# Shorter VectorE code, five transfers for the last values and 24 pad matmuls in a DMA-bound decode attention kernel

## The chip, the cores and the metric

The kernel runs on 1 core of one Trainium2 chip. The metric is the device time of one execution in microseconds (us). The kernel before takes 441.15 us (median of 3 runs, 440.98 to 441.19).

Engines: PE does matmuls (PEld is its weight load), DVE is VectorE, ACT is ScalarE, POOL is GpSimd, SP issues most of the transfers.

## The reference

Two attention blocks of a decode step, A and B: 4 sequences, 1 new token, 32 query heads on 8 key/value heads of 128, 8192 cached positions. A attends to all positions, B to the last 2048. The outputs are joined.

```python
q = (x @ wq).reshape(B, Sq, Hq, Dh).transpose(0, 2, 1, 3)      # D = 512, Hq*Dh = 4096
k, v = repeat(k_cache, 4), repeat(v_cache, 4)                   # B: only the last 2048 positions
p = softmax(einsum("bhqd,bhkd->bhqk", q, k) * Dh ** -0.5)
out = einsum("bhqk,bhkd->bhqd", p, v).reshape(B, Sq, Hq * Dh) @ wo
```

Everything is bf16. The caches of A are 2 x 64 MB and the used part of B's is 2 x 16 MB, so some 184 MB have to come in from memory for little arithmetic.

## The kernel before

The work is 20 units: 4 for B, then 16 for A, each with 4 MB of keys and 4 MB of values. PE transposes a unit's keys, computes scores, and runs the PV product of the unit before it. Two units make a turn; PE's code for a turn stands once, in a loop of 10 turns. DVE and ACT have their first three turns unrolled and then a loop. The last unit's PV and the last part of the output projection stand behind the loop (the tail).

At the start DVE sets masks and evacuates the small matmuls that make q:

```python
        def pe_job_xT(P):
            idx = xt_idx[P] = new_job("xT", "dve")
            ...
            def efn(dve):
                return dve.tensor_copy(out=xT[:, P, :, :],
                                       in_=bk[:, 0:DC * 8].rearrange("p (c b) -> p c b", c=DC)[:, :, 0:Bn])
        # pe_job_QP: one copy per job, 8 jobs.  pe_job_perm: four copies per job, 2 jobs.   (cut)

        def dve_setup0(dve):            # 4 memsets of MK; dve_setup1: 4 of MASK[0]; dve_setup2: 4 copies for permE
            mkv = MK[:, :].rearrange("p (g s h) -> p g s h", g=NSEG, s=2)
            dve.memset(mkv[0:64, :, 0, :], 0.0)
            ...
        op("dve", dve_setup0, inc=("mk0",))
```

POOL clears buffers and makes the identity matrices, which release PE's first instruction. Each step of DVE's softmax chain has a semaphore of its own (`max`, `maxc`, `sum`, `rcp`, `os`), on which later DVE steps wait.

The tail; each `c` is 16 matmuls of the last unit L:

```python
        VCH = [4, 2, 1, 1]                                  # V of the last unit in four transfers: 2, 1, 0.5, 0.5 MB
        vch_of = [i for i, n in enumerate(VCH) for _ in range(n)]
        for c in range(NC):                                 # NC = 8
            w = [("VL", vch_of[c])]
            if c == 0:
                w.append(("exp", L, 0))
            if c == 4:
                pe_SM(L)                                    # 16 matmuls for the softmax sums
                op("pe", pe_seed, waits=[("ocp", NTURN - 1)])
            pe_PV(L, c, bank=KTB[0], waits=w)
        add_norm(L, bank=KTB[0])
        # then 16 projection matmuls, two for each of eight 128 KB loads of Wl, which come last in the queue
```

Of the kernel before, what the change touches and what calls it, by code (L numbers as in the profile page):

```python
# [9 lines left out]
ACTF = mybir.ActivationFunctionType  # L10
# [4 lines left out]
def bass_concat_heads__gqa_block_cached__sliding_block_cached__decode_kernel(  # L15
# [15 lines left out]
    Bn, _, D = A_x.shape  # L31
    _, HKV, SK, DH = A_k_cache.shape
# [6 lines left out]
    NSEG = 4  # L39
# [31 lines left out]
    with ExitStack() as es:  # L71
# [8 lines left out]
        def sm(name):  # L80
# [39 lines left out]
        KTB = [ps("KT%d" % i, 512) for i in range(NBK)]  # L120
        OTB = ps("OT", 512)

        names = ["k0", "k1", "kh", "v0", "v1", "vl0", "vl1", "vl2", "vl3", "wl0", "wl1", "wl2", "wl3", "wl4", "wl5", "wl6", "wl7", "x0", "x1", "w0", "w1", "wo",
                 "out0", "out1", "out2", "Tq", "Td", "Ta", "S", "PV", "Ed", "Ea", "Eq", "max", "sub", "sum", "rcp", "exp", "otr", "os", "otp",
                 "ocp", "Ef", "fin0", "fin1", "ar1", "SM", "maxc", "pset", "setup", "pm0", "pm1", "oc", "ocB", "mk0", "mk", "mka", "perm", "rq"]
        sems = {n: sm("s_" + n) for n in names}

        K_sbf = K_sb.bitcast(F32)
# [6 lines left out]
        def sem_of(key):  # L135
            t = key[0]
            if t in ("K", "Kh"):
                return sems["k%d" % (key[1] % 2)]
            if t in ("V", "Vh"):
                return sems["v%d" % (key[1] % 2)]  # L140
            if t == "T":
                j = jobs[key[1]]
                return sems["Tq" if j["turn"] is None else "Td" if j["eng"] == "dve" else "Ta"]
            if t == "pm":
                return sems["pm%d" % key[2]]
            if t == "KH":
                return sems["kh"]
            if t in ("VL", "WL", "x", "out", "fin"):
                return sems["%s%d" % (t.lower(), key[1])]
            if t == "WQ":  # L150
                return sems["w%d" % key[1]]
            if t == "E":
                if jobs[key[1]]["turn"] is None:
                    return sems["Eq"]
                return sems["Ed"] if jobs[key[1]]["eng"] == "dve" else sems["Ea"]
            return sems[t]

        DMA_KEYS = ("K", "Kh", "KH", "V", "Vh", "VL", "WL", "x", "out", "WQ", "wo", "mk")

# [10 lines left out]
        def add(d):  # L170
            op(d["eng"], d["fn"], waits=d["waits"], inc=d["inc"])
# [16 lines left out]
            return KTB[jobs[idx]["bank"]]  # L188

        def pe_job_xT(P):  # L190
            idx = xt_idx[P] = new_job("xT", "dve")
            bk = kbank(idx).bitcast(BF16)

            def fn(pe):
                ins = None
                for c in range(DC):
                    ins = pe.transpose(out=bk[:, c * 8:c * 8 + Bn], in_=x_sb[0:Bn, P, :].rearrange("b (p c) -> b c p", c=DC)[:, c, :],  # L197
                                       identity=ident[0:Bn, 0:Bn])
                return ins
            op("pe", fn, waits=[("x", P), ("setup",), bankfree(idx)], inc=("T", idx))  # L200

            def efn(dve):
                return dve.tensor_copy(out=xT[:, P, :, :],
                                       in_=bk[:, 0:DC * 8].rearrange("p (c b) -> p c b", c=DC)[:, :, 0:Bn])
            add(dict(eng="dve", fn=efn, waits=[("T", idx)], inc=("E", idx)))

        def wq_view(P):
            return V_sb[:, 1 - P, :, :].rearrange("p t d -> p (t d)").rearrange("p (c n) -> p c n", c=DC)

        def pe_job_QP(P, i):  # L210
            idx = qp_idx[(P, i)] = new_job("QP", "dve")
            bk = kbank(idx)
            wv = wq_view(P)

            def fn(pe):
                ins = None
                for hl in range(HQJ):
                    hq = i * HQJ + hl
                    for c in range(DC):
                        ins = pe.matmul(out=bk[:, hl * Bn:(hl + 1) * Bn], lhsT=wv[:, c, hq * DH:(hq + 1) * DH],  # L220
                                        rhs=xT[:, P, c, :], start=(c == 0), stop=(c == DC - 1))
                return ins
            op("pe", fn, waits=[("WQ", P), ("E", xt_idx[P]), bankfree(idx)], inc=("T", idx))

            def efn(dve):
                return dve.tensor_copy(out=QT[:, P, :, i * HQJ:(i + 1) * HQJ],
                                       in_=bk[:, 0:HQJ * Bn].rearrange("p (h b) -> p b h", b=Bn))
            add(dict(eng="dve", fn=efn, waits=[("T", idx)], inc=("E", idx)))

        def pe_job_perm(P):  # L230
            idx = perm_idx[P] = new_job("perm", "dve")
            bk = kbank(idx)

            def fn(pe):
                ins = None
                for e in range(2):
                    ins = pe.matmul(out=bk[:, e * Bn * HQ:(e + 1) * Bn * HQ],
                                    lhsT=permE[:, e, :, :].rearrange("p t i -> p (t i)"),
                                    rhs=QT[:, P, :, :].rearrange("p b h -> p (b h)"), start=True, stop=True)
                return ins  # L240
            op("pe", fn, waits=[("E", qp_idx[(P, NQP - 1)]), ("perm",), bankfree(idx)], inc=("T", idx))

            def efn(dve):
                ins = None
                for e in range(2):
                    for tl in range(2):
                        src = bk[64 * tl:64 * tl + 64, e * Bn * HQ:(e + 1) * Bn * HQ]
                        ins = dve.tensor_copy(
                            out=RQ[P][64 * tl:64 * tl + 64, :, :, e, C * tl:C * tl + C],
                            in_=src.rearrange("p (b g c) -> p b g c", b=Bn, g=NSEG))  # L250
                return ins
            add(dict(eng="dve", fn=efn, waits=[("T", idx)], inc=("E", idx)))

        def pe_filler(n):
            bank = (jobs[-1]["bank"] + 1) % NBK
# [103 lines left out]
        def pe_job_OL(tn):  # L359
            idx = ol_idx[tn] = new_job("OL", "dve")  # L360
            bk = kbank(idx)

            def fn(pe):
                ins = None
                for r in range(REP):
                    ins = pe.matmul(out=bk[:, r * NR:(r + 1) * NR], lhsT=ORx[:, r, :, :].rearrange("p h m -> p (h m)"),
                                    rhs=ident[0:NR, 0:NR], start=True, stop=True)
                return ins
            op("pe", fn, waits=[("E", ot_idx[tn]), bankfree(idx)], inc=("T", idx))

            def efn(dve):
                ins = None
                for h in range(REP):
                    ins = dve.tensor_copy(
                        out=OL[32 * h:32 * h + 32, :, :, :],
                        in_=bk[32 * h:32 * h + 32, 0:REP * NR].rearrange("p (r g h b) -> p g h r b", r=REP, g=2, h=REP)[:, :, h, :, :])
                return ins
            return dict(eng="dve", fn=efn, waits=[("T", idx)], inc=("E", idx))
# [125 lines left out]
        def pool_otp(tn):  # L504
# [5 lines left out]
                w.append(("otr", 2 * tn - 2))  # L510
            return dict(eng="pool", fn=lambda pool: pool.tensor_copy(out=OTp[:, :, :], in_=OT_sb[:, P, q, :, :]), waits=w, inc=("otp", tn))

        def pool_setup0(pool):
            pool.memset(dummy[:, :], 0.0)
            pool.memset(onesf[:, :], 1.0)
# [4 lines left out]
            pool.memset(oacc[:, :], 0.0)  # L520
            pool.memset(PT[:, :, :], 0.0)
            return pool.memset(Wo_sb[:, :, :, :], 0.0)
        op("pool", pool_setup0, inc=("pset",))

        def pool_setup1(pool):
            ins = pool.affine_select(out=ident[:, :], in_=onesb[:, :], pattern=[[1, 128]],
# [3 lines left out]
            return ins  # L530
        op("pool", pool_setup1, waits=[("pset",)], inc=("setup",))

        def dve_setup0(dve):
            mkv = MK[:, :].rearrange("p (g s h) -> p g s h", g=NSEG, s=2)
            dve.memset(mkv[0:64, :, 0, :], 0.0)
            dve.memset(mkv[0:64, :, 1, :], -BIG)
            dve.memset(mkv[64:128, :, 0, :], -BIG)
            return dve.memset(mkv[64:128, :, 1, :], 0.0)
        op("dve", dve_setup0, inc=("mk0",))

        def dve_setup1(dve):
            dve.memset(MASK[0][0:64, 0:REP], 0.0)
            dve.memset(MASK[0][0:64, REP:C], -BIG)
            dve.memset(MASK[0][64:128, 0:REP], -BIG)
            return dve.memset(MASK[0][64:128, REP:C], 0.0)
        op("dve", dve_setup1, inc=("mka",))

        def dve_setup2(dve):
            ins = None
            for e in range(2):  # L550
                for tl in range(2):
                    ins = dve.tensor_copy(out=permE[:, e, tl, :], in_=ident[:, :].rearrange("p (i e) -> p e i", e=2)[:, e, :])
            return ins
        op("dve", dve_setup2, waits=[("setup",)], inc=("perm",))
        for sh in range(2):
            m0 = MASK[1][:, :]
            pstm = m0.ap[0][0]
# [13 lines left out]
        def act_warm(act):  # L571
            return act.activation(out=dummy[:, 1:2], in_=dummy[:, 0:1], func=ACTF.Exp)
        op("act", act_warm, waits=[("setup",)])

        for P in (1, 0):
            pe_job_xT(P)
# [102 lines left out]
            return ins  # L679
        add(dve_sum(L))  # L680
        add(dve_rcp(L))
        VCH = [4, 2, 1, 1]
        vch_of = [i for i, n in enumerate(VCH) for _ in range(n)]
        for c in range(NC):
            w = [("VL", vch_of[c])]
# [246 lines left out]
```

## Time and profile before

| | value |
|---|---|
| time, median of 3 | 441.15 us |
| span of the profiled run | 439.6 us |
| bytes, mean rate over the span | 184.76 MB, 420 GB/s |
| DMA rate from 200 to 300 us | 431 GB/s |
| busy share PE, DVE, ACT | 83%, 48%, 43% |
| idle of PE between the loop and the tail | 1.36 us |
| stall of PE among the last projections (start to start, less the usual 0.11 us) | 0.66 us |

Lines of the page of before: busy time by engine (us, share, instructions), the DMA packets, the chain of work that ended last by engine, and two lines of the DMA issues (count, KB each, median us from issue to landing).

```profile
PE 365.9 (83%) x7302; PEld 338.4 (77%) x7312; DVE 210.1 (48%) x462; ACT 189.7 (43%) x203; POOL 27.8 (6%) x84
...
DMA packets 13253, 184.76 MB, mean 420 GB/s; under 512 B 1412, under 2 KB 2488, under 8 KB 4536
...
DMA 46%; PE 45%; PEld 4%; issue 2%; DVE 1%; SPq 1%; PEldq 0%
...
K_sb<-in_A_k_cache_dram SPq DMA_DIRECT2D x15, 4096.0 KB, 22.8
V_sb<-in_A_v_cache_dram SPq DMA_DIRECT2D x15, 4096.0 KB, 30.6
```

PE, DVE and ACT all have idle time. The 4 MB loads land 22.8 and 30.6 us after issue; at 430 GB/s (an estimate from the table below) 4 MB take 9.8 us, so each load waits in a filled queue.

The table of stretches of before: for each stretch its length, busy us and instruction count of PE, PEld, DVE, ACT and POOL, granted PE clock, DMA share, GB/s.

```profile
core 0: us, PE busy (x) PEld busy (x) DVE busy (x) ACT busy (x) POOL busy (x), PEclk, DMA share, GB/s
40.00:100.00 60.00, 57.46 (x1177) 53.89 (x1179) 33.64 (x65) 33.78 (x36) 2.24 (x7) 1.00 1.02 424
...
200.00:300.00 100.00, 84.77 (x1620) 79.30 (x1619) 49.41 (x106) 45.02 (x48) 4.39 (x17) 0.91 1.00 431
...
430.00:440.00 10.00, 6.63 (x141) 4.90 (x137) 1.22 (x4) 0.37 (x1) 0.00 (x0) 1.00 0.49 173
```

The DMA engines run at a share of 1.00 to 1.02 from 40 to 400 us.

The timeline of before at the start (start us, us, engine, line, instruction, and in brackets the idle time before it and what ended that): the issue of the first V loads, and PE's first transpose of keys.

```profile
24.33 4.81 SPq L566 DMA_DIRECT2D V_sb<-in_B_v_cache_dram  x4
...
34.54 3.28 PEld L278 LDWEIGHTS KT<-identf,K_sb 128*128 128x128 f32 x16 [4.01 <-DMA K_sb<-in_B_k_cache_dram]
```

PE waits 4 us for the first keys, so the startup chain has that much to spare.

The timeline of PE in the tail of before: the last unit's PV (x64 are 64 matmuls), sums, second PV half, and the second to the fifth of the 16 projections with the stall.

```profile
429.17 1.98 PE L325 MATMUL KT<-PT,V_sb 128*128 128x64 bf16 x64 [1.36 <-DMA V_sb<-in_A_v_cache_dram]
431.01 0.63 PE L337 MATMUL SA<-PT,onesb 128*128 128x64 bf16 x16
...
432.52 2.04 PE L325 MATMUL KT<-PT,V_sb 128*128 128x64 bf16 x64
...
434.98 0.27 PE L699 MATMUL SA<-Wl_sb,OT_sb 128*4 128x256 bf16 x1
435.09 0.27 PE L699 MATMUL KT<-Wl_sb,OT_sb 128*4 128x256 bf16 x1
435.86 0.27 PE L699 MATMUL SA<-Wl_sb,OT_sb 128*4 128x256 bf16 x1 [0.50 <-issue]
435.97 0.27 PE L699 MATMUL KT<-Wl_sb,OT_sb 128*4 128x256 bf16 x1
```

Projections start 0.11 us apart, but the fourth starts 0.77 us after the third: a stall of 0.66 us, put down to "issue", which means that the profile shows no wait. No semaphore is waited for at this place in the code.

### The profile page before, as it was taken

How to read it: one execution, taken by the hardware profiler on the slowest of the kernel's cores; microseconds unless marked ns; L12 is line 12 of the kernel's file. 1: busy time of each engine (PE TensorE's matmuls, PEld its weight loads, DVE VectorE, ACT ScalarE, POOL GpSimd, SP SyncE). 2: the span in 40 equal slices, each digit the busy share in tenths (PEclk: the TensorE clock that was granted, in tenths of full speed). 3: DMA queues.
4: the chain of work that ended last, by engine and by line, in shares of the span. 5: the costliest groups of instructions: out<-in, count | busy, mean ns of one | idle time of the engine just before them, and what ended most of it. 6: DMA issues, size and time to landing. Idle time of an engine off the chain costs nothing.

```text
span 439.6 us, 15842 instructions
## 1 busy us (share of the span) xinstructions
PE 365.9 (83%) x7302; PEld 338.4 (77%) x7312; DVE 210.1 (48%) x462; ACT 189.7 (43%) x203; POOL 27.8 (6%) x84
## 2 busy tenths in 40 slices
PE   0168998998997969896989698969868895989986
PEld 0158897997996959795979688968868795979965
DVE  0034455654664633563546346625643563546641
ACT  1004473573563524361635254534534361635630
POOL 6100000000000000000000000000100000000000
PEclk9999999999999897998899799989997999899999
DMA  8999999999999999999999999999999999999995
GB/s 335 429 415 419 420 416 423 420 439 413 441 432 432 419 438 432 429 427 432 441 432 426 430 435 424 435 432 432 407 451 429 432 427 432 429 429 412 447 404 209
DMA packets 13253, 184.76 MB, mean 420 GB/s; under 512 B 1412, under 2 KB 2488, under 8 KB 4536
## 3 DMA queue, kind: packets, MB, share of 16 engines
q1 hardware_dynamic: 13152, 184.56, 98.9%
q8 instruction: 8, 0.13, 0.1%
q14 instruction: 5, 0.04, 0.0%
q0 software_dynamic: 64, 0.02, 0.0%
q10 hardware_dynamic: 24, 0.01, 0.0%
HBM read 184.56 MB, written 0.01 MB: 420 GB/s over the span
## 4 chain that ended last, share of the span: by engine, by line
DMA 46%; PE 45%; PEld 4%; issue 2%; DVE 1%; SPq 1%; PEldq 0%
DMA K_sb<-in_A_k_cache_dram 35%; PE KT L278 23%; PE OT L325 9%; DMA K_sb<-in_B_k_cache_dram 7%; DMA V_sb<-in_A_v_cache_dram 4%; PE SA L309 4%; PE SB L309 4%; PE KT L387 3%; PEld KT L278 2%; SPq L566 1%; PE SA L337 1%; PE KT L325 1%; DVE oacc L395 1%; PEld OT L325 1%; PEld SA L309 1%
## 5 line engine op out<-in xcount | busy, mean ns | idle before, releaser
L278 PE MATMUL KT<-identf,K_sb 128*128 128x128 f32 x1280 | 208.7, 297 | 44.1 <-DMA K_sb<-in_A_k_cache_dram 30.6
L287 ACT ACTIVATE KT_sb<-KT 128x1024 bf16<-128x1024 bf16 x160 | 163.3, 1024 | 138.0 <-PE KT L278 138.0
L278 PEld LDWEIGHTS KT<-identf,K_sb 128*128 128x128 f32 x1280 | 148.0, 150 | 49.7 <-DMA K_sb<-in_A_k_cache_dram 31.8
L286 DVE COPY KT_sb<-KT 128x512 int32<-128x512 int32 x160 | 110.5, 690 | 120.8 <-PE KT L278 119.5
L325 PE MATMUL OT<-PT,V_sb 128*128 128x64 bf16 x2560 | 78.1, 193 | 2.1 <-DMA V_sb<-in_A_v_cache_dram 1.2
L325 PEld LDWEIGHTS OT<-PT,V_sb 128*128 128x128 bf16 x2560 | 75.9, 98 | 2.3 <-DMA V_sb<-in_A_v_cache_dram 1.3
L460 ACT ACTIVATE PT<-Dt 128x512 bf16<-128x512 f32 x40 | 24.6, 630 | 80.4 <-DVE Dt L449 80.4
L309 PEld LDWEIGHTS SA<-RQc,KT_sb 128*128 128x128 bf16 x1280 | 57.2, 98 | 2.5
L309 PEld LDWEIGHTS SB<-RQc,KT_sb 128*128 128x128 bf16 x1280 | 50.5, 97 | 7.9 <-issue 4.4
L309 PE MATMUL SA<-RQc,KT_sb 128*128 128x16 bf16 x1280 | 56.4, 170 | 0.0
L309 PE MATMUL SB<-RQc,KT_sb 128*128 128x16 bf16 x1280 | 52.8, 170 | 0.0
L411 DVE TENSOR_REDUCE M<-SB 128x8 f32<-128x512 f32 (+1 forms) x20 | 13.8, 692 | 50.3 <-PE SB L309 50.3
L432 POOL PARTITION_ALL_REDUCE MB<-M1m x20 | 7.7, 386 | 335.1 <-DVE M1m L425 335.1
L387 PE MATMUL KT<-Wo_sb,OL 128*4 128x512 bf16 x80 | 18.9, 379 | 0.0
L197 PE MATMUL KT<-ident,x_sb 4*128 4x4 bf16 x8 | 0.5, 169 | 20.1 <-POOL identf L528 20.1
L197 PEld LDWEIGHTS KT<-ident,x_sb 4*128 4x128 bf16 x8 | 0.4, 111 | 20.3 <-issue 20.3
L449 DVE TENSOR_TENSOR Dt<-SA,MBm 128x512 f32<-128x512 f32 x20 | 13.8, 691 | 0.7
L449 DVE TENSOR_TENSOR Dt<-SB,MBm 128x512 f32<-128x512 f32 x20 | 13.6, 681 | 0.0
L411 DVE TENSOR_REDUCE M<-SA 128x8 f32<-128x512 f32 (+1 forms) x20 | 13.6, 681 | 0.0
L337 PE MATMUL SA<-PT,onesb 128*128 128x64 bf16 x336 | 13.2, 192 | 0.0
L387 PEld LDWEIGHTS KT<-Wo_sb,OL 128*4 128x4 bf16 x80 | 6.0, 84 | 8.1
L337 PEld LDWEIGHTS SA<-PT,onesb 128*128 128x128 bf16 x336 | 11.1, 97 | 0.0
(72 smaller groups left out, 123.1 us busy)
## 6 DMA issues: line engine op xcount, KB each, us to landing
K_sb<-in_A_k_cache_dram SPq DMA_DIRECT2D x15, 4096.0 KB, 22.8
V_sb<-in_A_v_cache_dram SPq DMA_DIRECT2D x15, 4096.0 KB, 30.6
K_sb<-in_B_k_cache_dram SPq DMA_DIRECT2D x16, 1024.0 KB, 22.5
V_sb<-in_B_v_cache_dram SPq DMA_DIRECT2D x16, 1024.0 KB, 19.4
V_sb<-in_B_wq_dram SPq DMA_DIRECT2D x1, 4096.0 KB, 12.5
V_sb<-in_A_wq_dram SPq DMA_DIRECT2D x1, 4096.0 KB, 22.0
Wo_sb<-in_B_wo_dram SPq DMA_DIRECT2D x4, 1024.0 KB, 11.3
K_sb<-in_A_k_cache_dram SPq DMA_DIRECT2D x2, 2048.0 KB, 18.6
```

The costliest lines, as they stand in the source:

```text
L278: ins = pe.transpose(out=bkf[:, pi * 128:(pi + 1) * 128], in_=K_sbf[:, slot, t0:t0 + 2, :].rearrange("p t d -> p (t d)"), identity=identf[ ...
L286: return e.tensor_copy(out=KT_sb.bitcast(I32)[:, tj % NKT, :], in_=bkf.bitcast(I32)[:, :])
L287: return e.activation(out=KT_sb[:, tj % NKT, :], in_=bk[:, :], func=ACTF.Copy)
L309: ins = pe.matmul(out=stb[:, t % NTH * C:(t % NTH + 2) * C], lhsT=ktv[:, pi, :, e], rhs=RQc[:, u % 2, t // TS, e, :], start=(e == 0), stop ...
L325: ins = pe.matmul(out=otb[:, s * NW:s * NW + w], lhsT=V_sb[:, slot, t, :], rhs=PT[:, slot, t * C:t * C + w], start=(j == 0), stop=(j == n ...
L337: ins = pe.matmul(out=SA[u % 2][:, s * NW:(s + 1) * NW], lhsT=onesb[:, :], rhs=PT[:, u % 2, c0:c0 + NW], start=(i == 0), stop=(i == n - 1))
L387: ins = pe.matmul(out=bk[0:Bn, 0:D], lhsT=OL[:, i // REP, i % REP, :], rhs=Wo_sb[:, i // REP, i % REP, :], start=(i == 0), stop=(i == C - 1))
L395: return dve.tensor_tensor(out=oacc[:, :], in0=bk[0:Bn, 0:D], in1=oacc[:, :], op=AluOpType.add)
L411: return dve.tensor_reduce(out=M1[:, h * n:(h + 1) * n].rearrange("p (s h) -> p s h", h=C), in_=bank[:, :].rearrange("p (s j h) -> p s h j ...
L432: return pool.partition_all_reduce(MB[:, 0:n], M1m[:, 0:n], channels=128, reduce_op=ReduceOp.max)
L449: return dve.tensor_tensor(out=Dt[:, h * NTH * C:(h + 1) * NTH * C].rearrange("p (s j h) -> p s j h", s=Sh, h=C), in0=bank[:, :].rearrange ...
L460: return act.activation(out=PT[:, u % 2, a:b], in_=Dt[:, a:b], func=ACTF.Exp, scale=scale)
```

## The change

The intent is to shorten VectorE's code and to let the last PV start earlier. The diff, cut to its core:

```diff
-            idx = xt_idx[P] = new_job("xT", "dve")                 # same for QP and perm
+            idx = xt_idx[P] = new_job("xT", "act")
...
-                return dve.tensor_copy(out=xT[:, P, :, :], ...)
+                return act.activation(out=xT[:, P, :, :], ..., func=ACTF.Copy)
...
-                for e in range(2):                                 # perm: four copies on DVE
-                    for tl in range(2):
-                        ins = dve.tensor_copy(...)
+                for tl in range(2):                                # two on ACT
+                    ins = act.activation(..., func=ACTF.Copy)
...
+                if tn not in pieces:                               # first three turns: one copy, not four
+                    return dve.tensor_copy(out=OL[...], in_=bk[:, 0:NR])
...
-            return sems[t]
+            return sems["vs" if t in ("max", "maxc", "sum", "rcp", "os") else t]
...
-        op("dve", dve_setup0, inc=("mk0",))                        # 8 memsets and permE
+        op("pool", pool_mask0, inc=("mk0",))                       # now first on POOL
...
+        def pe_pad(pe):
+            for _ in range(24):
+                ins = pe.matmul(out=KTB[NBK - 1][:, 0:Bn], lhsT=ident[:, :], rhs=ident[:, 0:Bn], start=True, stop=True)
+            return ins
+        op("pe", pe_pad, waits=[("setup",)])                       # ahead of all of PE's other work
...
-        VCH = [4, 2, 1, 1]
+        VCH = [2, 2, 2, 1, 1]
```

The results of the pads are never read.

More of the change, by code (lines that the diff above doesn't have):

```diff
@@ L121, in bass_concat_heads__gqa_block_cached__sliding_block_cached__decode_kernel @@
         OTB = ps("OT", 512)
-        names = ["k0", "k1", "kh", "v0", "v1", "vl0", "vl1", "vl2", "vl3", "wl0", "wl1", "wl2", "wl3", "wl4", "wl5", "wl6", "wl7", "x0", "x1", "w0", "w1", "wo",
-                 "out0", "out1", "out2", "Tq", "Td", "Ta", "S", "PV", "Ed", "Ea", "Eq", "max", "sub", "sum", "rcp", "exp", "otr", "os", "otp",
-                 "ocp", "Ef", "fin0", "fin1", "ar1", "SM", "maxc", "pset", "setup", "pm0", "pm1", "oc", "ocB", "mk0", "mk", "mka", "perm", "rq"]
+        names = ["k0", "k1", "kh", "v0", "v1", "vl0", "vl1", "vl2", "vl3", "vl4", "wl0", "wl1", "wl2", "wl3", "wl4", "wl5", "wl6", "wl7", "x0", "x1", "w0", "w1", "wo",
+                 "out0", "out1", "out2", "Tq", "Td", "Ta", "S", "PV", "Ed", "Ea", "Eq", "vs", "sub", "exp", "otr", "otp",
+                 "ocp", "Ef", "fin0", "fin1", "ar1", "SM", "pset", "setup", "pm0", "pm1", "oc", "ocB", "mk0", "mk", "mka", "perm", "rq"]
         sems = {n: sm("s_" + n) for n in names}
@@ L200, in pe_job_xT, with efn @@
             op("pe", fn, waits=[("x", P), ("setup",), bankfree(idx)], inc=("T", idx))
-            def efn(dve):
-                return dve.tensor_copy(out=xT[:, P, :, :],
-                                       in_=bk[:, 0:DC * 8].rearrange("p (c b) -> p c b", c=DC)[:, :, 0:Bn])
-            add(dict(eng="dve", fn=efn, waits=[("T", idx)], inc=("E", idx)))
+            def efn(act):
+                return act.activation(out=xT[:, P, :, :],
+                                      in_=bk[:, 0:DC * 8].rearrange("p (c b) -> p c b", c=DC)[:, :, 0:Bn], func=ACTF.Copy)
+            add(dict(eng="act", fn=efn, waits=[("T", idx)], inc=("E", idx)))
         def wq_view(P):
@@ L210, in pe_job_QP @@
         def pe_job_QP(P, i):
-            idx = qp_idx[(P, i)] = new_job("QP", "dve")
+            idx = qp_idx[(P, i)] = new_job("QP", "act")
             bk = kbank(idx)
@@ L223, in pe_job_QP, with efn @@
             op("pe", fn, waits=[("WQ", P), ("E", xt_idx[P]), bankfree(idx)], inc=("T", idx))
-            def efn(dve):
-                return dve.tensor_copy(out=QT[:, P, :, i * HQJ:(i + 1) * HQJ],
-                                       in_=bk[:, 0:HQJ * Bn].rearrange("p (h b) -> p b h", b=Bn))
-            add(dict(eng="dve", fn=efn, waits=[("T", idx)], inc=("E", idx)))
+            def efn(act):
+                return act.activation(out=QT[:, P, :, i * HQJ:(i + 1) * HQJ],
+                                      in_=bk[:, 0:HQJ * Bn].rearrange("p (h b) -> p b h", b=Bn), func=ACTF.Copy)
+            add(dict(eng="act", fn=efn, waits=[("T", idx)], inc=("E", idx)))
         def pe_job_perm(P):
-            idx = perm_idx[P] = new_job("perm", "dve")
+            idx = perm_idx[P] = new_job("perm", "act")
             bk = kbank(idx)
@@ L241, in pe_job_perm, with efn @@
             op("pe", fn, waits=[("E", qp_idx[(P, NQP - 1)]), ("perm",), bankfree(idx)], inc=("T", idx))
-            def efn(dve):
+            def efn(act):
                 ins = None
-                for e in range(2):
-                    for tl in range(2):
-                        src = bk[64 * tl:64 * tl + 64, e * Bn * HQ:(e + 1) * Bn * HQ]
-                        ins = dve.tensor_copy(
-                            out=RQ[P][64 * tl:64 * tl + 64, :, :, e, C * tl:C * tl + C],
-                            in_=src.rearrange("p (b g c) -> p b g c", b=Bn, g=NSEG))
+                for tl in range(2):
+                    ins = act.activation(
+                        out=RQ[P][64 * tl:64 * tl + 64, :, :, :, C * tl:C * tl + C].rearrange("p b g e c -> p e (b g) c"),
+                        in_=bk[64 * tl:64 * tl + 64, 0:2 * Bn * HQ].rearrange("p (e s c) -> p e s c", e=2, c=C), func=ACTF.Copy)
                 return ins
-            add(dict(eng="dve", fn=efn, waits=[("T", idx)], inc=("E", idx)))
+            add(dict(eng="act", fn=efn, waits=[("T", idx)], inc=("E", idx)))
         def pe_filler(n):
@@ L371, in efn @@
             def efn(dve):
+                if tn not in pieces:
+                    return dve.tensor_copy(out=OL[:, :, :, :].rearrange("p g r b -> p (g r b)"), in_=bk[:, 0:NR])
                 ins = None
@@ L511, in pool_otp, with pool_mask0, pool_mask1 @@
             return dict(eng="pool", fn=lambda pool: pool.tensor_copy(out=OTp[:, :, :], in_=OT_sb[:, P, q, :, :]), waits=w, inc=("otp", tn))
+        def pool_mask0(pool):
+            mkv = MK[:, :].rearrange("p (g s h) -> p g s h", g=NSEG, s=2)
+            pool.memset(mkv[0:64, :, 0, :], 0.0)
+            pool.memset(mkv[0:64, :, 1, :], -BIG)
+            pool.memset(mkv[64:128, :, 0, :], -BIG)
+            return pool.memset(mkv[64:128, :, 1, :], 0.0)
+        op("pool", pool_mask0, inc=("mk0",))
+        def pool_mask1(pool):
+            pool.memset(MASK[0][0:64, 0:REP], 0.0)
+            pool.memset(MASK[0][0:64, REP:C], -BIG)
+            pool.memset(MASK[0][64:128, 0:REP], -BIG)
+            return pool.memset(MASK[0][64:128, REP:C], 0.0)
+        op("pool", pool_mask1, inc=("mka",))
         def pool_setup0(pool):
@@ L522, in pool_setup0 @@
             return pool.memset(Wo_sb[:, :, :, :], 0.0)
-        op("pool", pool_setup0, inc=("pset",))
+        op("pool", pool_setup0, waits=[("mk0",), ("mka",)], inc=("pset",))
         def pool_setup1(pool):
@@ L531, in bass_concat_heads__gqa_block_cached__sliding_block_cached__decode_kernel, with pool_perm @@
         op("pool", pool_setup1, waits=[("pset",)], inc=("setup",))
-        def dve_setup0(dve):
-            mkv = MK[:, :].rearrange("p (g s h) -> p g s h", g=NSEG, s=2)
-            dve.memset(mkv[0:64, :, 0, :], 0.0)
-            dve.memset(mkv[0:64, :, 1, :], -BIG)
-            dve.memset(mkv[64:128, :, 0, :], -BIG)
-            return dve.memset(mkv[64:128, :, 1, :], 0.0)
-        op("dve", dve_setup0, inc=("mk0",))
-        def dve_setup1(dve):
-            dve.memset(MASK[0][0:64, 0:REP], 0.0)
-            dve.memset(MASK[0][0:64, REP:C], -BIG)
-            dve.memset(MASK[0][64:128, 0:REP], -BIG)
-            return dve.memset(MASK[0][64:128, REP:C], 0.0)
-        op("dve", dve_setup1, inc=("mka",))
-        def dve_setup2(dve):
+        def pool_perm(pool):
             ins = None
@@ L551, in dve_setup2 @@
                 for tl in range(2):
-                    ins = dve.tensor_copy(out=permE[:, e, tl, :], in_=ident[:, :].rearrange("p (i e) -> p e i", e=2)[:, e, :])
+                    ins = pool.tensor_copy(out=permE[:, e, tl, :], in_=ident[:, :].rearrange("p (i e) -> p e i", e=2)[:, e, :])
             return ins
-        op("dve", dve_setup2, waits=[("setup",)], inc=("perm",))
+        op("pool", pool_perm, waits=[("setup",)], inc=("perm",))
         for sh in range(2):
@@ L573, in bass_concat_heads__gqa_block_cached__sliding_block_cached__decode_kernel @@
         op("act", act_warm, waits=[("setup",)])
+        def pe_pad(pe):
+            ins = None
+            for _ in range(24):
+                ins = pe.matmul(out=KTB[NBK - 1][:, 0:Bn], lhsT=ident[:, :], rhs=ident[:, 0:Bn], start=True, stop=True)
+            return ins
+        op("pe", pe_pad, waits=[("setup",)])
         for P in (1, 0):
```

## The prediction

> **What bounds the kernel now.** The DMA engines. The page counts 184.76 MB in a span of 439.6 us, 420 GB/s on average. The table of stretches shows 424 to 431 GB/s at a DMA share of 1.00 to 1.02 from 40 to 400 us; only the first 10 us (342 GB/s) and the last 10 us (173 GB/s) are below. The Trainium skill, "Perfetto Trace Analysis", section Roofline, puts the ceiling of one core's 16 DMA engines at about 435 GB/s; this trace agrees. DVE is busy 48%, ACT 43%, PE 83%, and PE's transposes waited 30.6 us for keys of A. The loads have slack: 4 MB K loads land 22.8 us after issue, though 4 MB at 430 GB/s take 9.8 us (an estimate), so about 13 us of loads are queued ahead. A compute engine a few us faster or slower changes when a load is queued, not when it lands.
>
> **What the change moves.**
> - DVE's work at the start: 8 memsets of 0.07 us, 4 copies for permE (0.50), 2 xT copies of 0.16, 8 QT copies of 0.19, 2 x 1.20 for RQ: about 5 us of 210. ACT gets the evacuations at about the same cost (its smallest instruction took 0.20 us, a 4x256 one 0.37), GpSimd the memsets and permE.
> - In the first three turns OL is one copy instead of four of 0.20 us.
> - One chain semaphore: fewer semaphore instructions in DVE's loop.
> - 24 pads on PE: 128 such matmuls took 3.56 us, so about 0.7 us (estimate), after the GpSimd setup that ends at 20.0 us.
> The startup chain gets 1 to 2 us longer. It ends about 32 us; PE then waits 3.7 us for the first keys, landing at 34.5: hidden. The V load it releases (24.33) queues behind loads landing until about 40 us: hidden.
>
> **The tail.** After the first V chunk (2 MB) lands at 428.75, PE does 64 matmuls (1.98 us), sums and seed (1.4), then 64 more (2.0) to 434.56. With 1 MB chunks the first half starts near 427.8, so PE is about 1 us ahead. But the last 0.5 MB chunk lands only near 433.9 (22.8 us after issue), and its matmuls take 0.5 us: the end moves to about 434.4 at best. The last Wl load lands near 436.4; its matmuls run from 437.06, so at most 0.6 us is there. A stall of 0.5 to 0.8 us between projection matmuls at 435.1, put down to "issue", has no wait in the program; I take it for an instruction fetch. The Trainium skill, "Runtime: NRT & Kernel Launch", section Instruction fetch mechanics, gives blocks of 256 instructions; no view here shows the fetch. The pads move later block boundaries by some 48 instructions, so the stall may go where PE waits anyway.
>
> **Prediction.** 440.9 us, range 440.0 to 441.7. Faster by over 2%: 1%; within 2%: 98%; slower: 1%.
>
> **What would show it.** DVE busy down by 5 to 8 us, ACT up by 3 to 5; the DMA rate of 40 to 400 us unchanged within 1%; first K transposes still near 34.5 us after a wait; the last V chunk within 0.5 us of 433.9; the last unit's PV starting earlier but ending within 0.4 us of before; final matmul within 0.7 us.
>
> **What would make it wrong.** A GpSimd startup longer by far more than 0.5 us, so that the DMA queue runs dry; another DMA rate between builds; five V transfers delaying the Wl loads.

## More of the kernel before

One line of the DMA view of before, cut to 432 to 434.8 us: the queue that loads instructions for PE (packets, MB, share of the engines).

```profile
q8 instruction: 1, 0.02, 2.5%
```

In those 2.8 us one packet of instructions was loaded.

## The result

| | before | after |
|---|---|---|
| time, median of 6 runs | 441.17 us (440.98 to 441.62) | 441.63 us (441.15 to 443.01) |
| span of the profiled run | 439.6 us | 440.2 us |
| DVE busy, ACT busy | 210.1, 189.7 us | 203.5, 193.0 us |
| first matmul of the tail | 429.17 us | 428.59 us |
| stall in the tail (start to start, less the usual step) | 0.66 us, after the third projection | 1.85 us, after 44 of the 64 matmuls of the second PV half |
| last projection starts | 437.17 us | 437.80 us |

The ratio of after to before is 1.0013, 95% interval 0.9999 to 1.0028: the same within 2%, and 0.13% on the slow side. A ratio is the mean time of one kernel's runs over that of the other's of the same rounds, so it is not quite the ratio of the medians. All outputs are right.

The page of after, busy time and packets:

```profile
PE 368.2 (84%) x7336; PEld 340.1 (77%) x7336; DVE 203.5 (46%) x423; ACT 193.0 (44%) x217; POOL 29.0 (7%) x96
...
DMA packets 13396, 184.75 MB, mean 420 GB/s; under 512 B 1428, under 2 KB 2504, under 8 KB 4552
```

The table of stretches of after, same columns as before:

```profile
40.00:100.00 60.00, 57.96 (x1180) 53.94 (x1179) 32.36 (x59) 33.58 (x36) 2.23 (x7) 1.00 1.02 424
...
200.00:300.00 100.00, 84.47 (x1560) 78.83 (x1556) 47.65 (x100) 44.99 (x48) 4.01 (x16) 0.90 1.00 431
...
430.00:440.00 10.00, 6.06 (x122) 4.46 (x118) 1.22 (x4) 0.37 (x1) 0.00 (x0) 1.00 0.50 179
```

The DMA rate is the same. From the packets of the data queue (184.56 MB) in the traces I added up the bytes: 184.5 MB had been moved at 434.83 us in before and at 434.94 us in after.

The timeline of after at the start: the pads, the first V loads, the first transposes.

```profile
21.13 0.80 PE L578 MATMUL KT<-ident 128*128 128x4 bf16 x24 [21.13 <-POOL identf L543]
...
26.11 3.19 SPq L566 DMA_DIRECT2D V_sb<-in_B_v_cache_dram  x4
...
34.16 3.27 PEld L276 LDWEIGHTS KT<-identf,K_sb 128*128 128x128 f32 x16 [2.20 <-DMA K_sb<-in_B_k_cache_dram]
```

The startup chain is 1.8 us longer (V issued at 26.11 instead of 24.33), and PE still waits 2.2 us for the keys.

The timeline of PE in the tail of after:

```profile
428.59 1.98 PE L323 MATMUL KT<-PT,V_sb 128*128 128x64 bf16 x64 [1.36 <-issue]
...
431.94 1.46 PE L323 MATMUL KT<-PT,V_sb 128*128 128x64 bf16 x44
435.09 0.76 PE L323 MATMUL KT<-PT,V_sb 128*128 128x64 bf16 x20 [1.69 <-issue]
436.16 0.27 PE L706 MATMUL KT<-Wl_sb,OT_sb 128*4 128x256 bf16 x1 [0.32 <-issue]
436.27 0.27 PE L706 MATMUL SA<-Wl_sb,OT_sb 128*4 128x256 bf16 x1
```

The first line still comes after 1.36 us of idle time, now with no wait for V. The stall among the projections is gone, but there is one in the middle of the second PV half, again with nothing waited for. The bracket gives it 1.69 us, counted from the end of the matmul before; from start to start, less the usual 0.03 us, it is 1.85 us. Counted by brackets the stall of before is 0.50 us.

The DMA view of after, 432 to 434.8 us, PE's instruction queue:

```profile
q8 instruction: 1, 0.02, 2.5%
```

### The profile page after: what moved, and what is told of

The parts are those of the page before. It is cut to its first block, busy times and chain, and to the rows that moved or that the text cites. A ratio compares the mean times of both kernels' runs of the same rounds, so it can differ in the third digit from the quotient of the medians.

```text
span 440.2 us, 15841 instructions
## 1 busy us (share of the span) xinstructions
PE 368.2 (84%) x7336; PEld 340.1 (77%) x7336; DVE 203.5 (46%) x423; ACT 193.0 (44%) x217; POOL 29.0 (7%) x96
## 3 DMA queue, kind: packets, MB, share of 16 engines
q1 hardware_dynamic: 13296, 184.56, 98.8%
HBM read 184.56 MB, written 0.01 MB: 419 GB/s over the span
## 4 chain that ended last, share of the span: by engine, by line
DMA 48%; PE 46%; issue 2%; SPq 2%; DVE 1%; PEld 1%; PEldq 0%
DMA K_sb<-in_A_k_cache_dram 34%; PE KT L276 23%; PE OT L323 9%; DMA K_sb<-in_B_k_cache_dram 7%; DMA V_sb<-in_A_v_cache_dram 7%; PE SB L307 4%; PE SA L307 4%; PE KT L387 3%; SPq L566 1%; PE SA L335 1%; PE KT L323 1%; DVE oacc L395 1%; PEld OT L323 1%; DVE OS L492 0%; PE KT L259 0%
```

## The experiments

Names: "b" kernels start from before, "a" kernels from after; "pad24" is the number of pad matmuls, "v4" the old four V transfers, "dve44" 44 memsets put in at DVE's start. "a_dve" is after without pads and with four V transfers.

The theories, as the expectations name them:

- **F**: the stall is a fetch of PE's instructions, and the pads move the block boundary at which it happens. The Trainium skill, "Runtime: NRT & Kernel Launch", section Instruction fetch mechanics, says that the sequencer refills its instruction memory in 16 KiB blocks of 256 instructions, ahead of use and mostly hidden; PE's packets of instructions here have 16384 bytes. **F1**: the fetch of a block starts when PE enters the block ahead of it. **F2**: it starts when the loop is left.
- **S**: the split of V, or the moved DVE work, costs the time.
- **W** (formed later): the moved DVE work pays because DVE's code needs one instruction fetch less.

Times are ratios to before of the same rounds; an interval of about 0.0013 to either side belongs to each.

### b_pad24: the pads alone

```diff
 # before, ahead of the first pe_job_xT
+        op("pe", pe_pad, waits=[("setup",)])      # 24 matmuls
```

> The kernel before with the 24 pad matmuls as its only change. Theory F (the pads move an instruction-block boundary in PE's code, so that the stall of 0.5 us among the last projections becomes one of about 1.7 us in the last unit's PV): the stall appears after some 44 to 46 matmuls of the second PV half, the projections run without a gap, and the time is that of after: 0.4 to 1.2 us over before. Rival S (the split of the last V, or the moved DVE work, costs the time): within 0.2 us of before and the stall stays among the projections.

Measured: 443.14 us median (442.51 to 444.74), ratio 1.0044 (1.0030 to 1.0058). The timeline of PE in its tail:

```profile
432.75 1.46 PE L325 MATMUL KT<-PT,V_sb 128*128 128x64 bf16 x44
435.91 0.76 PE L325 MATMUL KT<-PT,V_sb 128*128 128x64 bf16 x20 [1.70 <-issue]
...
437.15 0.42 PE L706 MATMUL SA<-Wl_sb,OT_sb 128*4 128x256 bf16 x1
```

The stall stands at the same matmul as in after, with nothing but the pads changed: S falls for this part. The size is a miss: I expected 0.4 to 1.2 us over before and the median rose by 2.05 us. Part of that is in the third line: a projection takes 0.42 us here instead of 0.27, and they start 0.21 us apart instead of 0.11. The table of stretches of this run (columns as above) shows why:

```profile
437.00:439.00 2.00, 2.00 (x10) 1.21 (x11) 0.00 (x0) 0.00 (x0) 0.00 (x0) 0.50 0.00 0
```

The granted clock was 0.50 from 437 to 439 us. Before had its next such stretch only at 440.96 us, after the end of its work. This run, the slowest of the five at 444.74 us, was late enough to fall into one. Whether the other four fell in too is not shown.

### a_pad0: after without the pads

```diff
-        op("pe", pe_pad, waits=[("setup",)])
```

> The kernel after without its pads. Theory F: the stall is back among the projections (one matmul earlier or later, as one more wait stands ahead of it), about 0.5 us long; the time is within 0.3 us of before. Rival S: still 0.5 us or more over before.

Measured: 440.36 us, ratio 0.9984 (0.9970 to 0.9997). The timeline of PE among the projections, third to fifth:

```profile
434.36 0.27 PE L699 MATMUL KT<-Wl_sb,OT_sb 128*4 128x256 bf16 x1
434.55 0.27 PE L699 MATMUL SA<-Wl_sb,OT_sb 128*4 128x256 bf16 x1
434.66 0.27 PE L699 MATMUL KT<-Wl_sb,OT_sb 128*4 128x256 bf16 x1
```

The boundary is back behind the third projection, and the stall is only 0.08 us (0.19 us instead of 0.11 between the third and the fourth). The time is 0.7 us under before, more than I expected. The pads are what makes after slower; what is left of the change gains a little.

### a_pad40: 40 pads instead of 24

```diff
-            for _ in range(24):
+            for _ in range(40):
```

> The kernel after with 40 pads instead of 24. Two forms of theory F part here. F1, the fetch of a block starts when PE enters the block ahead of it: with 40 pads that block begins some 15 matmuls before the end of the loop, so the fetch is made in the loop's first pass; no stall in the tail, no instruction fetch after 100 us, and 0.5 us or more under before. F2, the fetch starts when the loop is left: the stall stays, ends about 6.5 us after the tail's first matmul as now, but comes 16 matmuls earlier, so the time is about 0.5 us over that of after.

Measured: 440.20 us, ratio 0.9985 (0.9972 to 0.9999). No stall. The traces' instruction packets for PE: before and after load seven blocks between 25 and 72 us and the next at 433.33 and 432.55 us. This kernel loads an eighth at 75.96 us, in the loop, and the next one only at 435.32 us, too late to be needed. F2, by which the stall stays, falls; the run agrees with F1, but for that late packet, which I had not expected. With 40 pads in place of 24 the time is less.

What binds the end now is seen in the timeline of PE among the projections, the twelfth to the fifteenth:

```profile
435.26 0.27 PE L706 MATMUL SA<-Wl_sb,OT_sb 128*4 128x256 bf16 x1
435.46 0.27 PE L706 MATMUL KT<-Wl_sb,OT_sb 128*4 128x256 bf16 x1
435.57 0.27 PE L706 MATMUL SA<-Wl_sb,OT_sb 128*4 128x256 bf16 x1
435.89 0.27 PE L706 MATMUL KT<-Wl_sb,OT_sb 128*4 128x256 bf16 x1
```

The thirteenth starts 0.20 us after the twelfth and the fifteenth 0.32 us after the fourteenth, instead of 0.11; each of the two is the first that needs a further Wl load. The last Wl load lands at 435.84 us in this trace: the projections wait for the DMA engines.

### a_dve: the moved DVE work and the chain semaphore alone

```diff
-        op("pe", pe_pad, waits=[("setup",)])
-        VCH = [2, 2, 2, 1, 1]
+        VCH = [4, 2, 1, 1]
```

> The kernel after without pads and with the old four V transfers: the moved VectorE work and the chain semaphore alone. All theories but one: within 0.3 us of before, with DVE busy about 6 us less. If the moved work itself costs (later start of the chain), 0.5 us or more over before.

Measured: 440.79 us, ratio 0.9993 (0.9979 to 1.0007): unclear by itself. Its trace has the first matmul of the tail at 428.64 us, 0.53 us before that of before, and its stall, 0.37 us, behind the third projection.

### b_pad40: before with 40 pads

```diff
 # before, ahead of the first pe_job_xT
+        op("pe", pe_pad, waits=[("setup",)])      # 40 matmuls
```

> The kernel before with 40 pads. Theory F1 (block fetch starts when PE enters the block ahead; with 40 pads that is inside the loop): no stall in the tail, one block fetch more near 76 us and none between 420 and 434 us, and the time 0.4 to 0.9 us under before. If instead the gain of the 40-pad version of after came from the moved DVE work or the split: within 0.3 us of before.

The timeline of PE in the tail, and PE's instruction queue at 74 to 78 us:

```profile
432.34 2.04 PE L325 MATMUL KT<-PT,V_sb 128*128 128x64 bf16 x64
434.70 0.27 PE L706 MATMUL KT<-Wl_sb,OT_sb 128*4 128x256 bf16 x1 [0.32 <-issue]
434.81 0.27 PE L706 MATMUL SA<-Wl_sb,OT_sb 128*4 128x256 bf16 x1
```

```profile
q8 instruction: 1, 0.02, 1.7%
```

The trace is as F1 has it: no stall, one block more at 75 us, last projection at 436.52 us (437.17 in before). The time is a miss: 441.02 us, ratio 0.9996 (0.9984 to 1.0009), where I expected 0.4 us or more under before. The interval reaches 0.7 us under it, so this run doesn't settle the size.

### b_split: the five V transfers alone

```diff
-        VCH = [4, 2, 1, 1]
+        VCH = [2, 2, 2, 1, 1]
```

> The kernel before with the five V transfers alone. If PE's start on the last unit is bound by leaving the loop (1.36 us idle in every trace so far, whatever the size of the first V transfer): that idle stays 1.36 us, and the time is within 0.2 us of before. If the split gives what the kernel without pads gained over the one with four transfers: 0.4 us under before.

Measured: 441.21 us, ratio 0.9995 (0.9982 to 1.0008). The first line of the tail:

```profile
429.41 1.98 PE L325 MATMUL KT<-PT,V_sb 128*128 128x64 bf16 x64 [1.36 <-issue]
```

The idle time before the tail is 1.36 us, as in before, after and every other trace but one (1.33 us in b_pad40_dve20). The first transfer of 1 MB landed at 426.58 us here, long before. PE was not held up by V at this place. The profile had put the wait of before down to the V load because that came last. The same idle time stands between two turns inside the loop, here before the transposes of a turn:

```profile
393.95 2.10 PE L278 MATMUL KT<-identf,K_sb 128*128 128x128 f32 x16 [1.36 <-issue]
```

The records of the trace of before show what fills it: at the end of a turn the program lowers eight semaphores, one instruction each 0.15 us (427.62 to 428.73 us), then come the loop's counter and its branch. This end of a turn has a fixed length, and so has the whole way to the tail: in all fifteen traces the tail's first matmul starts 5.29 to 5.32 us after V of the unit before the last has landed (3.9 us of its PV matmuls, then the end of the turn). That V, and not V of the last unit, sets when the tail begins.

### a_pad40_v4: 40 pads, four V transfers

```diff
-            for _ in range(24):
+            for _ in range(40):
-        VCH = [2, 2, 2, 1, 1]
+        VCH = [4, 2, 1, 1]
```

> 40 pads, moved DVE work, but the old four V transfers. If the split is worth nothing: the same as with five transfers and 40 pads, 440.2 to 440.5 us. If it is worth 0.4 us: about 440.7.

Measured: 440.16 us, ratio 0.9977 (0.9965 to 0.9989). It is not slower than with five transfers: no worth of the split is seen, here or in b_split, though the intervals leave some 0.5 us either way. This is the fastest version found, 0.23% under before and clear of it, but not clear of a_pad0 (0.9984) or a_pad40 (0.9985).

### a_pad12: 12 pads

```diff
-            for _ in range(24):
+            for _ in range(12):
```

> The kernel after with 12 pads. Theory F1: the boundary falls 12 matmuls later than with 24, some 8 matmuls before the end of the second PV half; the stall stands there and is 0.8 to 1.5 us, between that of 0 pads (under 0.1 to 0.4) and of 24 (1.7); the time lies between 440.4 (0 pads) and 441.8 (24 pads). If the pads cost by their own time at the start and not by the boundary: no stall at that place.

Measured: 441.25 us, ratio 1.0001 (0.9988 to 1.0014). PE's second PV half:

```profile
431.51 1.83 PE L323 MATMUL KT<-PT,V_sb 128*128 128x64 bf16 x56
434.67 0.41 PE L323 MATMUL KT<-PT,V_sb 128*128 128x64 bf16 x8 [1.33 <-issue]
```

Twelve pads fewer than in after, and the stall comes 12 matmuls later and is shorter. Table of all ten traces (us; the packet's end from the instruction packets in the traces; the stall from start to start, less the usual 0.11 us of projections or 0.03 us of PV matmuls, which is 0.16 us more than the brackets say):

| kernel | pads | first matmul of the tail | place of the stall | stall | packet ends | PE goes on | last projection starts |
|---|---|---|---|---|---|---|---|
| before | 0 | 429.17 | after projection 3 | 0.66 | 434.45 | 435.86 | 437.17 |
| b_split | 0 | 429.41 | after projection 3 | 0.54 | 434.66 | 436.03 | 437.34 |
| a_dve | 0 | 428.64 | after projection 3 | 0.37 | 433.60 | 435.13 | 436.44 |
| a_pad0 | 0 | 428.38 | after projection 3 | 0.08 | 433.19 | 434.55 | 435.96 |
| a_pad12 | 12 | 428.16 | after 56 of 64 | 1.50 | 433.24 | 434.67 | 437.02 |
| b_pad24 | 24 | 429.40 | after 44 of 64 | 1.87 | 434.44 | 435.91 | 440.14 |
| after | 24 | 428.59 | after 44 of 64 | 1.85 | 433.67 | 435.09 | 437.80 |
| b_pad40 | 40 | 428.99 | none | 0 | none | none | 436.52 |
| a_pad40 | 40 | 428.26 | none | 0 | none | none | 436.00 |
| a_pad40_v4 | 40 | 428.52 | none | 0 | none | none | 436.06 |

In all seven traces with a stall PE goes on 1.36 to 1.53 us after the packet's end. That is what a wait for the packet looks like. The distance fits too: between the loop's branch and the stall the trace of after has 257 records of PE's instructions and that of before 304, 47 apart, where 24 pads are 48. F is shown.

Why the stall grows as it moves to the front, argued with F1: a block holds 128 matmuls (each a weight load and a matmul, 256 instructions). With F1 the fetch starts as PE enters the block ahead. In before that is 128 matmuls ahead of the stall, some 23 matmuls into the tail, about 429.9 us (an estimate from 0.031 us a matmul), and the next block is usable 6.0 us later. PE needs 5.2 us for the block, because it holds the sums, the seed and the wait for the last normalization. In after the block begins at the very start of the tail, 428.59 us, is usable 6.5 us later, and PE runs through it in 4.8 us. With 40 pads the block begins in the loop, so that its successor is fetched in the first pass and stays. The instant that starts a fetch is not shown: in the seven traces the packet starts 3.0 to 4.0 us after the entry so counted, and, more evenly, 3.7 to 4.2 us after the tail's first matmul. The end of the loop alone is not it, since in a_pad40 the packet starts 7.1 us after that matmul.

### a_pad40_v4_dve44, b_pad40_dve20, b_pad40_dve40: DVE's instruction fetches

One thing was open. The tail of every "a" kernel above began 0.35 to 1.25 us before that of every "b" kernel, though the bytes moved by a given time were the same. The traces hold, for each load into 128 partitions, 16 semaphore increments. The Trainium skill, "DMA: Bandwidth & Descriptors", section Why a DMA increments its semaphore by 16 and not by 1, says that each DMA engine of a transfer adds one when its own share has landed; the 16 increments per load in these traces agree. The time from the first to the last of them tells how far the latest DMA engine is behind the earliest. In before this spread is 2.16 us for a load landing at 142.88 us and 2.80 us for the one landing at 155.84 us, and it stays near 2.8 us until the last Wl loads. In a_dve it is 2.40 and 2.42 us. In before it is the latest of the 16 that falls back (2.16 to 2.80 us after the first); the one before it goes from 1.88 to 2.10 us. In between, at 152.3 us, before loads an 8 KB packet of instructions that a_dve does not. The trace doesn't say for which engine. Hence W, and these edits, which lengthen DVE's code alone:

```diff
+        dpad = sb("dpad", [128, 64], F32)
+        def dve_pad(dve):
+            for i in range(44):                       # 20, 40 in the others
+                ins = dve.memset(dpad[:, i:i + 1], 0.0)
+            return ins
+        op("dve", dve_pad)
```

> The fastest version so far (moved DVE work, 40 pads, four V transfers: 440.2 us) with 44 one-column memsets of an unused tile put back at the start of VectorE's code, while it has nothing else to do (about 0.06 us each). Theory W (the moved DVE work pays because VectorE's code gets short enough to need one 8 KB instruction fetch less; the fetch at 152 us delays one of the 16 DMA engines by about 0.7 us, and every load after it lands that much later): a fetch returns at 145 to 185 us, the spread of the 16 completions of a load grows there by 0.5 us or more if it falls on the latest DMA engine, and the time is then 440.7 to 441.1 us. Rival (it pays because VectorE is busy for a shorter time or waits on fewer semaphores in the loop): no new fetch, spread unchanged, 440.0 to 440.4 us.

> The kernel before with 40 pads (441.0 us) and 20 such memsets at the start of VectorE's code. Theory W: the fetch that was at 152 us comes earlier (about 20 instructions, near 130 us), away from the first Wo load; if the loss depends on where it falls, the spread of the completions does not grow at 152 to 156 us and the time is 440.1 to 440.5 us; if every such fetch costs, the spread grows earlier and the time stays at 441.0. Rival: nothing changes but the start; 441.0 us and the jump of the spread at 152 to 156 us as before.

> The same with 40 memsets: the fetch moves to about 115 to 120 us. Theory W: as with 20. Rival: as before, jump at 152 to 156 us, 441.0 us.

Measured: 440.58, 440.70 and 440.52 us; ratios 0.9985 (0.9971 to 0.9999), 0.9986 (0.9973 to 1.0000), 0.9987 (0.9973 to 1.0000). The DMA view of a_pad40_v4_dve44 at 151 to 153 us shows the fetch that had come back (queue 1 are the data, queue 14 the instructions of other engines than PE):

```profile
q1 hardware_dynamic: 166, 0.71, 88.9%
q14 instruction: 1, 0.01, 1.0%
```

The spread widens in the loads that land next after the fetch, wherever that falls: with 44 memsets from 2.16 to 2.98 us after a fetch at 151.8 us; with 20 (on the b kernel) from 1.95 to 2.80 us after a fetch at 148.0; with 40 from 2.06 to 2.77 us in the load landing at 133.56 us, after a fetch at 128.5. The fetch belongs to DVE, since memsets of DVE alone move it, and with it the latest DMA engine falls back by about 0.7 us, most or all of which is still there at the end. The branch of my expectation in which the loss depends on where the fetch falls is wrong. So are the times: 440.58 us is just under the 440.7 to 441.1 expected for 44, and the other two lie 0.3 to 0.5 us under the 441.0 that follows from an undiminished loss. Differences of this size are within the intervals.

### a_pad40_v4_dve8 and a_pad40_v4_dve52: the size of that term, on one chip

```diff
-            for i in range(44):
+            for i in range(8):                        # 52 in the other
```

> A control for the memsets put back: 8 of them instead of 44, too few to bring the fetch at about 152 us back. Theory W: no such fetch, the spread of the 16 completions stays near 2.0 to 2.3 us after 156 us, the last Wl load lands near 435.9 us, and the time is 440.0 to 440.4 us. If memsets as such slow the kernel: over 440.4 us.

> The same with 52 memsets, on the same chip as the control. Theory W: a fetch between 140 and 152 us, the spread grows by 0.5 us or more in the load that is landing then, the last Wl load lands 0.3 to 0.7 us later than in the control, and the time is 0.2 to 0.7 us over the control's. If the later landing does not reach the time: equal to the control within 0.15 us.

Measured: 440.20 us (440.14 to 440.39), ratio 0.9979 (0.9965 to 0.9992), and 440.53 us (440.24 to 440.75), ratio 0.9985 (0.9971 to 0.9999). The DMA view of the kernel with 8 memsets at 151 to 153 us has no line of instructions:

```profile
q1 hardware_dynamic: 168, 0.74, 91.6%
```

Eight memsets cost nothing that is seen (440.20 against 440.16 us with none). With the fetch, at 148.0 us, the spread goes from 2.07 to 2.73 us, the last Wl load lands at 436.37 instead of 435.95 us, and the time is 0.32 us more (difference of the means). So the term is about 0.3 us in kernels whose end waits for Wl; from the scatter of these two sets of five times I work out a 95% interval of 0.1 to 0.6 us. It rests on this pair: the ratios to before overlap, and a_pad40, without the fetch, had 0.9985 too.

Worked out from the completions in the traces, us:

| kernels | DVE's fetch after 120 us | spread at 143 us | spread at 156 us | V of the unit before the last lands | last Wl lands |
|---|---|---|---|---|---|
| before | 152.3 | 2.16 | 2.80 | 423.86 | 436.49 |
| b_split | 152.4 | 2.44 | 3.23 | 424.10 | 436.79 |
| b_pad24 | 152.2 | 1.97 | 2.92 | 424.08 | 436.71 |
| b_pad40 | 151.7 | 2.19 | 2.75 | 423.68 | 436.36 |
| b_pad40_dve20 | 148.0 | 1.95 | 2.81 | 423.65 | 436.33 |
| b_pad40_dve40 | 128.5 | 2.77 | 2.78 | 423.59 | 436.25 |
| a_pad40_v4_dve44 | 151.8 | 2.16 | 2.98 | 423.73 | 436.38 |
| a_pad40_v4_dve52 | 148.0 | 2.07 | 2.73 | 423.69 | 436.37 |
| after | none | 2.05 | 2.05 | 423.28 | 436.01 |
| a_dve | none | 2.40 | 2.42 | 423.32 | 436.01 |
| a_pad0 | none | 2.07 | 2.08 | 423.07 | 435.80 |
| a_pad12 | none | 1.82 | 1.82 | 422.84 | 435.60 |
| a_pad40 | none | 1.97 | 1.97 | 422.95 | 435.84 |
| a_pad40_v4 | none | 2.21 | 2.22 | 423.20 | 435.91 |
| a_pad40_v4_dve8 | none | 2.14 | 2.15 | 422.95 | 435.95 |

The eight traces with the fetch have V landed at 423.59 to 424.10 us, the seven without at 422.84 to 423.32: no overlap, means 0.71 us apart.

## Why the prediction was right or wrong

- **The bound: right**, though I passed over 20 to 30 us, where before had 398 GB/s. The DMA rate of 40 to 400 us did not change (424 to 431 GB/s in both), and no edit in fifteen kernels moved the bytes by more than a few tenths of a us.
- **The startup: right.** The chain got 1.8 us longer (I said 1 to 2) and stayed hidden: the first transposes began at 34.16 us (34.54 before). DVE busy fell by 6.6 us (5 to 8 expected), ACT's rose by 3.3 (3 to 5).
- **The pads: wrong, and this turned the sign of the median.** The failed step is "The pads move later block boundaries by some 48 instructions, so the stall may go where PE waits anyway." The cause of the stall and the shift were right; what I didn't do is to count where the boundary would go. It went 23 matmuls forward into the second PV half, where nothing waits, and the stall grew from 0.66 to 1.85 us. The count was to be had: three projections and 20 of the 64 PV matmuls ahead of the old place. I also wrote that no view shows the fetch; the DMA view does, as a packet in PE's instruction queue. That I booked the pads as 0.7 us of hidden time at the start was true and beside the point.
- **"With 1 MB chunks the first half starts near 427.8, so PE is about 1 us ahead": wrong.** PE is idle for the 1.36 us of the turn's end before the tail with either size of the first transfer (b_split, 429.41 us). The split alone has ratio 0.9995. I took the wait for V in the profile at its word.
- **"The V load it releases (24.33) queues behind loads landing until about 40 us: hidden" and DVE's work as worth nothing: a term left out.** DVE's busy time is indeed worth nothing, but its code is: one fetch less, V of the unit before the last 0.7 us earlier in the traces, and 0.32 us (0.1 to 0.6) in the time where it was measured by itself.
- **"the end moves to about 434.4 at best": wrong.** PV of the last unit ended 1.3 us later than before (435.85 against 434.56), by the stall. The term for the last V chunk was off too: it landed at 433.35 us in after, not near 433.9, and in a_pad40, without the stall, PV ended at 433.67 us.
- **The bound on the gain by Wl: right.** With the stall gone, the end waits for the last Wl loads (a_pad40), as said; the last one lands at 436.01 us in after (436.4 predicted).

The sum for the profiled runs: the tail begins 0.58 us earlier (DVE's code), the stall costs 1.19 us more (pads), the split adds nothing. That makes +0.61 us, where the last projection came 0.63 us later; the median rose by 0.46 us, which is not clear of noise (ratio 0.9999 to 1.0028). I had predicted -0.25 us.

Left open: at which instant a fetch starts; why PE needs 1.4 us after a packet's end; why the latest DMA engine falls back by about 0.7 us with a packet of 8 KB, and why the other such packets (in before at 53.2, 111.5, 189.8 and 250.1 us) do not widen the spread. The one at 53.2 us is DVE's too: 20 and 40 memsets move it to 34.2 and 24.5 us. On which of the 16 engines a packet runs is not in these traces.

## What to carry to other kernels

In a kernel bound by transfers, straight code behind a loop can wait for its own instructions: look for a stall that the profile puts down to "issue" at a place without a wait, count the matmuls to it, and look for an instruction packet just ahead of it. An edit that adds or removes a few instructions anywhere ahead shifts that place, so try some paddings before you judge such an edit; here 24 pads cost time (b_pad24), and 40 took the stall away, though against no pads no gain in time is shown (0.9985 in a_pad40, 0.9984 in a_pad0). Where the last transfer ends the kernel, the latest DMA engine counts and not the mean rate, and instruction bytes are part of its load.

## What the Trainium skill lacked or had wrong

- "Runtime: NRT & Kernel Launch", Instruction fetch mechanics: it calls the crossing of a block mostly hidden, because instructions are issued slower than they are filled in. Here PE runs a block of 128 matmuls in 4.8 to 5.2 us and the next one is usable only about 5.5 to 6.5 us after the block ahead is entered (an estimate from the count of matmuls; seven traces), so up to 1.9 us show. It gives no latency for the fetch beside a full data queue: here the packet took 1.1 us, and PE went on 1.36 to 1.53 us after its end.
- The same section gives 16 KiB blocks for every engine. PE's packets agree (16384 bytes); those of the other engines were 8192 bytes here.
- "DMA: Bandwidth & Descriptors" does not say that an instruction packet can set the latest DMA engine back for the rest of a program: about 0.7 us with one packet of 8 KB, seen in the 16 completions of the later loads.
- No page that I read gives the pace of PE at semaphore instructions that stand alone: here eight at the end of a turn came 0.15 us apart, and with the loop's counter and branch PE was idle for 1.33 to 1.36 us before the tail (fifteen traces).
- Nothing to mend in "Perfetto Trace Analysis", Roofline: it gives about 435 GB/s for the 16 DMA engines of one core; the traces agree with 424 to 431.
